# A Nyström attention and sticky expert kernel: two batches put on one Newton chain, and all order tables written anew

## The chip, the cores and the metric

The kernel runs on one core of a Trainium2 chip. The metric is device time in microseconds (us) of one execution; the time before is the median of three. Engines are called as in the profile: PE (TensorE matmul), PEld (its weight loads), DVE (VectorE), ACT (ScalarE), POOL (GpSimd), SP (SyncE, which here only issues loads).

## The reference

There are 8 batches (B), 8 heads, 576 tokens (S) and a head width of 64. First comes Nyström attention with 32 landmarks, the means of 18 tokens each:

```python
q_lm = q.reshape(B, H, m, S // m, D).mean(axis=3)
k_lm = k.reshape(B, H, m, S // m, D).mean(axis=3)
A = sm(q, k_lm)          # sm: softmax of the scaled product
Bm = sm(q_lm, k_lm)      # 32 x 32 for each head
C = sm(q_lm, k)
Z = Bm.transpose(0, 1, 3, 2) / (norm1(Bm) * norminf(Bm) + 1e-06)
for _ in range(6):
    Z = 2 * Z - Z @ Bm @ Z
return A @ Z @ C @ v
```

The loop is a Newton iteration for the pseudo-inverse of `Bm`: six steps, each of which needs the one before it, on one 32x32 matrix for each head and batch. The attention's result, 576 rows of 512 numbers for each batch, then goes to a mixture of 8 experts. A token takes the expert with its own largest gate value, or, where a local gate is at least 0.5, the expert of the token before it; its output is `p[e] * (relu(x @ w1[e]) @ w2[e])`, with `w1` 512x1024 and `w2` 1024x512.

## The kernel before

Each batch has a piece of attention and an expert run. The expert run takes the expert that most tokens of the batch chose ("votes") and runs all 576 tokens through it; tokens that chose another one are gathered into an additional short run (the "slot"), which stands between batches 6 and 7. Products of the expert run are made in three terms, since both factors are split in a high and a low part: `ath`, `atl` of the attention, `gh`, `gl` of the first weights, `h` (its two halves) and `wh`, `wl` of the second weights. L737 multiplies the attention with the first weights into the "ph" banks; ACT (L746) makes the relu and DVE (L749, L752) its low half; L790 and L781 multiply `h` with the second weights into "py" and "pg". A product of L737 can only be written to a ph bank whose relu and low half are done. The first weights of a batch are not `w1` itself but `w1` multiplied by the attention's folded value matrix `wt`; that product is L694, eight long products (sixteen passes of 32 rows) for one half of the weights.

The expert run of a batch is cut in 16 chunks. The attention of later batches is put into it piece by piece: `PLANS[b]` holds, for each step of batch b in the order of `STEPS`, the chunk at which the step is emitted, counted from the start of the run of batch b-1 (`SECOND` and `FIRST` do it for batches 1 and 0, `SLOT_AT` for the slot, `G_AT` for L694, `W2_AT` for some loads). From this emitted order a list scheduler with a cost model sets the order of each engine's queue, which is then fixed. `in_row` ties matmuls together so that nothing is put between them; `one` gives, in turn, the three small PSUM banks in which all small products land.

The steps that the change touches: `norms` (scales `Bm`, transposes it to `bt`, and makes the factor `nrc`), `nf` (`newton_first`, L420 product and L424 sums) and `n0` to `n5` (`newton_step`, L432 product and L435 sum). A Newton step is one "trip" here: eight small products on PE (sixteen passes in the trace, 32x32 weights and 64 columns, 32 in the last step), then one DVE sum of 128x2x64. Before, a batch's state `et` moves on through four tiles `et0` to `et3` that all batches share in turn (`next_et`). Other names below: L482 are the scores of `A` (8 products for half a batch) and L487 turns them over, L304 the scores of `C` with L317 and L319 their exponentials, L331 transposes of `C`, L345 its product with `v`, L493 to L505 the softmax of `A`, L516 and L520 the split of its result in `ath` and `atl` (128x1152), L590 to L593 the votes, L241 and L242 the landmark sums, L671 the loads of the first weights.

Of the kernel before, what the change touches and what calls it, by code (L numbers as in the profile page):

```python
# [9 lines left out]
F32 = mybir.dt.float32  # L10
# [4 lines left out]
ALU = mybir.AluOpType  # L15
# [22 lines left out]
JOINT = 3  # L38

# [37 lines left out]
def nystrom_attn_then_sticky_moe(ctx, tc, qT, kT, v, wg, w12, out):  # L77
# [291 lines left out]
    ets = [const.tile([P, 2, 96], F32, name=f"et{i}") for i in range(4)]  # L369
# [3 lines left out]
    def next_et():  # L373

        ets.append(ets.pop(0))
        return ets[-1]

    def norms(b, st):
# [5 lines left out]
        et = st["et"] = next_et()  # L384
# [17 lines left out]
        nrc = st["nrc"] = sm.tile([P, 2], F32, name="nrc")  # L402
# [896 lines left out]
    SECOND = dict(v=3.6, q0=0.1, k0=0.6, c0=0.6, q2=0.1, k2=1.1, c1=1.6, norms=2.6, a0=6.1, nf=7.1, a1=7.1, t0=7.6,
        amax=7.6, n0=7.6, t2=7.6, n1=7.6, t4=7.6, aexp=8.6, n2=7.6, cv=7.6, n3=7.6, n4=8.1, anorm=8.6, n5=8.1, nw=8.1,  # L1300
        gw=8.1, aback=8.6, gates=8.6, nwt=12.6, votes=8.6, split=10.1, w1=8.6, w1b=9.7, fresh=10.1, sticky=11.1,
        chosen=14.6, own=21.1)
# [3 lines left out]
        2: (-13.9, -11.4, -10.4, -13.4, -7.9, -9.4, -7.9, -7.4, -7.4, -6.4, -7.4, -4.4, -2.4, -4.9, -1.4, -1.4, 1.6,  # L1306
            -0.4, -1.4, -0.4, 0.1, 0.1, 1.6, -2.4, 6.6, 5.1, 5.1, 6.1, 6.6, 6.6, 8.1, 13.6, 8.1, 8.1, 9.1, 13.6,
            14.6),
        3: (-23.4, -16.9, -20.9, -13.4, None, -14.4, -14.4, -13.4, -13.4, -9.9, -8.4, -8.9, -6.4, -7.9, -3.4, -7.9,
            -8.4, -6.4, -7.9, -3.4, -2.9, -3.9, -2.4, -2.4, 1.1, 1.6, 1.6, 1.6, 3.6, 4.1, 3.6, 4.6, 8.6, 4.6, 6.1,  # L1310
            12.1, 12.6),
# [132 lines left out]
```

## Time and profile before

| what | us |
|---|---|
| median of 3 runs | 471.43 (471.01, 471.43, 475.08) |
| the profiled execution | 472.64 |
| its span | 470.9 |
| PE busy in the span | 456.2 (97%) |
| DVE, ACT, POOL busy | 272.0, 203.4, 233.1 |
| granted clock, mean | 0.996 of 2.4 GHz |

The span is what the profile covers; the execution's own time is 1.7 us longer. Matmuls are pipelined: one starts before the last has ended, so the distance from start to start is what a matmul takes from PE's time, not its own duration. Such distances are read from the timeline of PE, where each line gives the start, the busy time of the group, and in brackets how long the engine was idle before it.

### The profile page before, as it was taken

To read this page: it belongs to the slowest core of one execution; us is meant where nothing else is said; L and a number is where in the kernel's file an instruction comes from. 1 tells how busy PE (TensorE), PEld (TensorE's weight loads), DVE (VectorE), ACT (ScalarE), POOL (GpSimd) and SP (SyncE) were. 2 spreads that over 40 slices of the span, in tenths; PEclk is the share of its full clock that TensorE was granted. 3 is DMA by queue.
4 is the path that set the end of the run, shared out by engine and by line. 5 is a ranking of instruction groups with operands and counts; after the bars stand their busy time and mean duration, and the time that the engine had idled before them with its cause. 6 is when DMAs were issued, how large, how long until landed. Compare 5 with 4: busy or idle time off the path is not lost.

```text
span 470.9 us, 12133 instructions
## 1 busy us (share of the span) xinstructions
PE 456.2 (97%) x4709; PEld 338.3 (72%) x4709; DVE 272.0 (58%) x825; ACT 203.4 (43%) x516; POOL 233.1 (50%) x364
## 2 busy tenths in 40 slices
PE   8989999999999999999999999999999999999995
PEld 3546667687776777767886677767885887778884
DVE  6897866876586548548633575338548933523231
ACT  2456245554344616355245634354333613555121
POOL 7187582395374508448613544055426864467000
PEclk9999999999999999999999999999999999999998
DMA  8993383991497227937842244333532911762011
GB/s 305 316 376 127 114 308 104 359 336 59 148 321 254 90 73 253 366 89 249 316 135 74 92 173 178 126 96 110 205 107 58 321 43 48 235 218 75 1 57 47
DMA packets 38717, 82.01 MB, mean 174 GB/s; under 512 B 3275, under 2 KB 4555, under 8 KB 37888
## 3 DMA queue, kind: packets, MB, share of 16 engines
q1 hardware_dynamic: 31920, 66.70, 41.4%
q10 hardware_dynamic: 5248, 9.44, 5.7%
q0 software_dynamic: 1488, 5.07, 2.8%
q8 instruction: 38, 0.62, 0.5%
q14 instruction: 23, 0.19, 0.1%
HBM read 66.29 MB, written 14.94 MB: 173 GB/s over the span
## 4 chain that ended last, share of the span: by engine, by line
PE 81%; DVE 7%; DMA 3%; ACT 3%; issue 2%; POOL 2%; SPq 0%; POOLq 0%; ACTq 0%; DVEq 0%
PE py L790 36%; PE ph L737 21%; PE pg L781 5%; PE ph L694 3%; PE one L432 2%; PE one L345 2%; DMA k_t<-kT 2%; PE one L482 2%; PE one L331 2%; DMA q_t<-qT 1%; PE one L304 1%; POOL t L241 1%; ACT ec L317 1%; PE one L570 1%; DVE h L749 1%
## 5 line engine op out<-in xcount | busy, mean ns | idle before, releaser
L790 PE MATMUL py<-wh,h 128*128 128x512 f32 x528 | 171.9, 402 | 0.2
L725 POOL TENSOR_TENSOR wl<-raw,wh 128x512 fp32r<-128x512 f32 x68 | 87.0, 1298 | 70.1 <-ACT wh L720 62.2
L790 PEld LDWEIGHTS py<-wh,h 128*128 128x128 f32 x528 | 95.5, 188 | 28.7 <-issue 7.0
L746 ACT ACTIVATE h<-ph 128x256 fp32r<-128x256 f32 (+2 forms) x136 | 54.6, 402 | 133.1 <-PE ph L737 111.2
L749 DVE SCALAR_TENSOR_TENSOR h<-ph,h 128x256 fp32r<-128x256 f32 (+1 forms) x136 | 55.6, 410 | 81.4 <-ACT h L746 80.2
L790 PE MATMUL py<-wl,h 128*128 128x512 f32 x264 | 90.7, 393 | 0.0
L737 PE MATMUL ph<-ath,gh 128*128 128x320 f32 (+1 forms) x256 | 79.9, 312 | 2.5 <-DVE h L749 1.5
L737 PE MATMUL ph<-atl,gh 128*128 128x320 f32 (+1 forms) x256 | 75.9, 297 | 0.4 <-DVE atl L530 0.4
L737 PE MATMUL ph<-ath,gl 128*128 128x320 f32 (+1 forms) x256 | 76.0, 297 | 0.0
L737 PEld LDWEIGHTS ph<-ath,gh 128*128 128x128 f32 x256 | 48.1, 188 | 19.9 <-issue 6.2
L790 PEld LDWEIGHTS py<-wl,h 128*128 128x128 f32 x264 | 49.5, 188 | 10.3 <-issue 0.8
L737 PEld LDWEIGHTS ph<-atl,gh 128*128 128x128 f32 x256 | 48.2, 188 | 4.2 <-DVE atl L530 0.7
L737 PEld LDWEIGHTS ph<-ath,gl 128*128 128x128 f32 x256 | 48.1, 188 | 0.5 <-issue 0.3
L720 ACT CAST wh<-raw 128x512 fp32r<-128x512 f32 x68 | 41.1, 630 | 9.2 <-DMA raw<-w 8.8
L811 ACT ACTIVATE ys<-py,pall 128x512 f32<-128x512 f32 x30 | 20.0, 689 | 11.5 <-DMA out<-ys 7.5
L494 POOL TENSOR_TENSOR sa<-sa,mxa 128x1152 f32<-128x1152 f32 x7 | 14.9, 2133 | 19.8 <-DVE mxa L493 19.7
L707 ACT CAST gh<-ph 128x512 fp32r<-128x512 f32 (+1 forms) x19 | 10.6, 564 | 28.0 <-PE pg L694 26.2
L241 POOL TENSOR_TENSOR t<-k_t 128x288 f32<-128x288 f32 x24 | 19.6, 838 | 5.7 <-DMA k_t<-kT 1.6
L781 PE MATMUL pg<-wl,h 128*128 128x512 f32 x56 | 22.4, 400 | 0.0
L241 POOL TENSOR_TENSOR t<-q_t 128x288 f32<-128x288 f32 x28 | 20.4, 748 | 3.7 <-DVE sk L242 1.3
L781 PE MATMUL pg<-wh,h 128*128 128x512 f32 x56 | 22.2, 397 | 0.0
L435 DVE TENSOR_TENSOR et<-one,et 128x128 f32<-128x128 f32 (+1 forms) x42 | 11.3, 270 | 15.1 <-PE one L432 14.9
(337 smaller groups left out, 726.2 us busy)
## 6 DMA issues: line engine op xcount, KB each, us to landing
raw<-w SPq DMA_DIRECT2D x68, 256.0 KB, 5.1
raw<-w SPq DMA_DIRECT2D x17, 1024.0 KB, 7.1
v_t<-v SPq DMA_DIRECT2D x8, 1024.0 KB, 6.7
out<-ys ACTq DMA_DIRECT2D x32, 256.0 KB, 2.9
q_t<-qT SPq DMA_DIRECT2D x6, 1152.0 KB, 5.5
k_t<-kT SPq DMA_DIRECT2D x6, 1152.0 KB, 8.4
ad<-sa POOLq DMA_DIRECT2D x8, 576.0 KB, 3.3
q_t<-qT SPq DMA_DIRECT2D x4, 576.0 KB, 8.0
```

Of the source, the lines that this page charges most:

```text
L241: nc.gpsimd.tensor_add(t9[:, i], src[:, a + i, :, 0:9], src[:, a + i, :, 9:18])
L435: nc.vector.tensor_tensor(out=half(new, 1), in0=half(pn, 1), in1=half(et, 2), op=ALU.add)
L494: nc.gpsimd.tensor_tensor(out=sa, in0=sa, in1=mx.unsqueeze(2).broadcast_to([P, 2 * NJ, M]), op=ALU.subtract)
L694: mm = nc.tensor.matmul(ps[g][32 * c:32 * c + 32, 0:n * P], w, w1[r, n * i:n * i + n, a * P:a * P + P], start=True, stop=True)
L720: cut = nc.scalar.copy(out=wh, in_=raw)
L725: nc.gpsimd.tensor_tensor(out=wl, in0=raw, in1=wh.bitcast(F32), op=ALU.subtract)
L737: mm = nc.tensor.matmul(hp, w[:, g, c], x[:, g, s0:s0 + n], start=(i == 0), stop=(i == 5))
L746: nc.scalar.activation(out=h[:, 0:e], in_=hp[:, 0:e], func=AF.Relu)
L749: nc.vector.scalar_tensor_tensor(out=h[:, 384:384 + m], in0=hp[:, 0:m], scalar=0.0, in1=h[:, 0:m].bitcast(F32), op0=ALU.max, op1=ALU.subtract)
L781: nc.tensor.matmul(yps[4], hs[ff][1], w, start=(ff == 0 and w is w2[ff][0]), stop=(ff == NC2 - 1 and w is w2[ff][1]))
L790: mms.append(nc.tensor.matmul(yps[full[i]], h[:, part + i * P:part + i * P + P], w, start=(f == 0 and part == 0 and w is wh), stop=(f == N ...
L811: nc.scalar.mul(out=ys, in_=yp, mul=st["pw"][:, k:k + 1])
```

## The change

Batches 4 and 5 share one Newton chain (`PAIR = {4:5}`). Their states lie side by side in one tile of four matrices' width (`[P, 4, 96]`, of which there are now three instead of four tiles of half the width), and their factors in one tile `nrc4`. The first product and the six steps are emitted once, with batch 4's steps: a trip has 16 products tied in a row and one sum of 128x4x64. Batch 5's seven entries in its plan become None. Any other batch swaps its state twice for each step and thereby updates it in place. All tables are written anew.

```diff
+PAIR = {4:5}
-    ets = [const.tile([P, 2, 96], F32, name=f"et{i}") for i in range(4)]
+    ets = [const.tile([P, 4, 96], F32, name=f"et{i}") for i in range(3)]
...
-    def next_et():
-
-        ets.append(ets.pop(0))
-        return ets[-1]
+    def next_et(b):
+        bs = sorted((b, partner.get(b, b)))
+        if b not in used:
...
+        else:
+            for x in bs:
+                used[x] = used[x][::-1]
+        for x in bs:
+            kept[x % 2] = used[x][0]
+            sts[x]["et"] = ets[used[x][0]][:, 2 * (x % 2):2 * (x % 2) + 2]
+        return ets[used[b][0]][:, 0:4] if b in PAIR else sts[b]["et"]
...
     def newton_step(b, st, k, meanwhile=None):
         n = 64 if k < 5 else 32
-        et = st["et"]
-        pn = chain(b).tile([P, 2, 64])
-        each_place(lambda g, r: nc.tensor.matmul(pn[r, g, 0:n], et[r, g, 32:64], et[r, g, 0:n], start=True, stop=True))
-        new = st["et"] = next_et()
+        w = 4 if b in PAIR else 2
+        et = ets[used[b][0]] if b in PAIR else st["et"]
+        pn = chain(b).tile([P, w, 64])
+        mms = []
+        for q in range(0, w, 2):
+            each_place(lambda g, r: mms.append(nc.tensor.matmul(
+                pn[r, q + g, 0:n], et[r, q + g, 32:64], et[r, q + g, 0:n], start=True, stop=True)))
+        if b in PAIR:
+            in_row(mms)
+        new = next_et(b)
...
-        4: (-25.4, -20.9, -19.4, -18.4, None, -16.9, -16.9, -15.9, -15.4, -15.4, -14.9, -14.4, -11.9, -12.4, -10.4,
-            -6.9, -8.4, -7.9, -5.9, -8.4, -6.4, -5.9, -4.9, -6.9, -4.9, -5.4, -5.4, -3.9, 2.6, 4.1, 2.6, 2.6, 4.6,
+        4: (-25.4, -21.9, -19.9, -18.4, None, -17.4, -18.9, -15.9, -15.4, -15.4, -4.9, -14.4, -11.9, -4.4, -10.4,
+            -6.9, -1.4, -7.9, -6.9, -1.9, -6.9, -0.4, -4.4, -0.4, -4.4, 1.1, 1.6, 2.1, 2.6, 4.6, 2.6, 1.6, 4.6, 3.1,
```

So batch 4's Newton steps move from chunks -14.9 to -5.4 to chunks -4.9 to 1.1. The order of PE is the same up to about 87 us of the trace of before, differs from there to about 246 us, and is again the same to the end but for two short stretches (near 285 and 416 us). PE runs the same set of products; DVE has six instructions fewer and POOL one. Three places show what moved; lines of the new file are numbered some 50 higher (L694 becomes L746, L432 L481, L435 L487, L520 L572, L737 L789, L749 L801, L790 L842, L331 L334, L345 L348).

PE, before, at batch 2's first weights (`raw`, L694; near 141 us of the trace):

```order
L694 MATMUL pg<-raw_2084,wt 32x512
L694 MATMUL ph<-raw_2084,wt 32x512
L432 MATMUL one<-et_176 32x64 x8
L345 MATMUL one<-v_t,ect 32x64 x40
L624 LDWEIGHTS er
L624 MATMUL one<-identb,er 128x5
L625 LDWEIGHTS er
L625 MATMUL one<-identb,er 128x5
L432 MATMUL one<-et_177 32x64 x8
L694 MATMUL pg<-raw_2084,wt 32x512
```

The same place after:

```order
L842 MATMUL py<-wh,h 128x512 x2
L842 MATMUL py<-wl,h 128x512 x2
L746 MATMUL ph<-raw_2072,wt 32x512
L746 MATMUL pg<-raw_2072,wt 32x512
L746 MATMUL ph<-raw_2072,wt 32x512
L746 MATMUL pg<-raw_2072,wt 32x512
L746 MATMUL ph<-raw_2072,wt 32x512
L746 MATMUL pg<-raw_2072,wt 32x512
L746 MATMUL ph<-raw_2072,wt 32x512
L746 MATMUL pg<-raw_2072,wt 32x512
L789 MATMUL ph<-ath,gh 128x256
```

Before, two Newton trips and the product with `v` stand between the fifth and the sixth of the eight products; after, the eight stand together.

DVE, before, at the split of batch 2's attention (`atl`, near 129 to 133 us; `et` is the Newton state of batch 3):

```order
L435 TENSOR_TENSOR et_178<-one,et_176 128x2x64
L592 MAX top<-tot 128x8
L593 MAX_INDEX regs<-top,tot 128x8
L502 TENSOR_REDUCE rsa<-sa 128x36
L749 SCALAR_TENSOR_TENSOR h<-ph,h 128x256 x2
L242 TENSOR_REDUCE sq<-t_2812 128x64
L503 TENSOR_SCALAR rsa<-rsa 128x36
L435 TENSOR_TENSOR et_179<-one,et_178 128x2x64
L618 TENSOR_SCALAR old<-one 5x128
L520 TENSOR_TENSOR atl<-at,ath 128x1152
```

The same place after:

```order
L644 MAX top<-tot 128x8
L645 MAX_INDEX regs<-top,tot 128x8
L801 SCALAR_TENSOR_TENSOR h<-ph,h 128x256 x2
L487 TENSOR_TENSOR et_177<-one,et_177 128x2x64
L572 TENSOR_TENSOR atl<-at,ath 128x1152
L554 TENSOR_REDUCE rsa<-sa 128x36
L245 TENSOR_REDUCE sq<-t_2644 128x64
L555 TENSOR_SCALAR rsa<-rsa 128x36
L487 TENSOR_TENSOR et_177<-one,et_177 128x2x64
```

Before, two Newton sums of batch 3 stand ahead of `atl`; after, the second one stands behind it and behind two reductions.

PE, before, at the end of batch 4's Newton steps (near 189 to 193 us; the L694 are batch 3's first weights):

```order
L790 MATMUL py<-wl,h 128x512
L432 MATMUL one<-et_179 32x64 x8
L345 MATMUL one<-v_t,ect 32x64 x40
L432 MATMUL one<-et_176 32x64 x8
L694 MATMUL ph<-raw_2913,wt 32x512
L694 MATMUL pg<-raw_2913,wt 32x512
```

After, at the next half of the same first weights:

```order
L789 MATMUL ph<-atl,gh 128x256
L789 MATMUL ph<-ath,gl 128x256
L842 MATMUL py<-wh,h 128x512 x2
L481 MATMUL one<-et_176 32x64 x16
L746 MATMUL ph<-raw_2872,wt 32x512
L746 MATMUL pg<-raw_2872,wt 32x512
```

Trips of 8 products that belonged to batch 4 alone have become trips of 16 for both batches, later in the program.

## Rows read from the trace of the kernel before

**Rows 1.** Windows: length; busy PE, PEld, DVE, ACT, POOL; clock; DMA share; GB/s.

```profile
87.00:246.00 159.00, 157.53 (x1817) 118.74 (x1818) 101.39 (x299) 74.73 (x186) 89.39 (x125) 1.00 0.61 211
```

**Rows 2.** Timeline of PE at batch 2's and batch 3's first weights.

```profile
141.07 0.61 PE L694 MATMUL ph<-raw,wt 64*32 64x512 f32 x1
...
142.07 0.43 PE L432 MATMUL one<-et 32*32 32x64 f32 x16
...
144.57 0.61 PE L694 MATMUL pg<-raw,wt 64*32 64x512 f32 x1
...
145.56 0.38 PE L737 MATMUL ph<-ath,gh 128*128 128x256 f32 x1
...
192.77 0.61 PE L694 MATMUL ph<-raw,wt 64*32 64x512 f32 x1
...
193.79 0.50 PE L790 MATMUL py<-wh,h 128*128 128x512 f32 x1
```

**Rows 3.** Timeline of PE at the scores of batch 5 and of an earlier batch.

```profile
50.50 0.71 PE L482 MATMUL one<-q_t,k_t 64*32 64x288 f32 x16
51.14 0.73 PE L790 MATMUL py<-wh,h 128*128 128x512 f32 x2
...
210.75 1.16 PE L482 MATMUL one<-q_t,k_t 64*32 64x288 f32 x18
212.10 0.71 PE L482 MATMUL one<-q_t,k_t 64*32 64x288 f32 x14 [0.19 <-DVE sa L487]
212.74 0.74 PE L570 MATMUL one<-at,wgc 128*32 128x160 f32 x16
```

**Rows 4.** Timeline of PE around one Newton trip of batch 5.

```profile
242.85 0.42 PE L432 MATMUL one<-et 32*32 32x64 f32 x16
243.21 0.50 PE L790 MATMUL py<-wh,h 128*128 128x512 f32 x1
```

**Rows 5.** The source line L432, all passes: duration ns min/median/max.

```profile
L432 PE MATMUL one<-et x672: 191/214/239, 59.2 to 354.5; 32*32 32x64 f32 x140, 32*32 32x32 f32 x28
```

**Rows 6.** Timeline of PE at a Newton trip of batch 3 in two pieces.

```profile
135.95 0.41 PE L432 MATMUL one<-et 32*32 32x64 f32 x12
136.30 0.50 PE L790 MATMUL py<-wh,h 128*128 128x512 f32 x1
...
137.88 0.30 PE L432 MATMUL one<-et 32*32 32x64 f32 x4
138.11 0.50 PE L790 MATMUL py<-wh,h 128*128 128x512 f32 x1
```

**Rows 7.** Timeline of PE at its longest wait between 87 and 246 us.

```profile
187.21 0.40 PE L790 MATMUL py<-wl,h 128*128 128x512 f32 x1
188.80 0.38 PE L737 MATMUL ph<-ath,gh 128*128 128x256 f32 x1 [1.19 <-DVE h L749]
```

**Rows 8.** Timeline of DVE and POOL at that wait.

```profile
185.47 2.94 DVE L520 TENSOR_TENSOR atl<-at,ath 128x1152 fp32r<-128x1152 f32 x1
...
186.48 2.53 POOL L241 TENSOR_TENSOR t<-k_t 128x288 f32<-128x288 f32 x2
```

**Rows 9.** The source line L520: duration ns min/median/max.

```profile
L520 DVE TENSOR_TENSOR atl<-at,ath x7: 1316/1349/2940, 80.8 to 375.0; 128x1152 fp32r<-128x1152 f32 x7
```

**Rows 10.** Timeline of DVE and ACT behind the scores of batch 3.

```profile
110.01 0.21 DVE L311 TENSOR_REDUCE mx<-ph 128x1 f32<-128x64 f32 x1
...
111.01 0.28 ACT L319 ACTIVATE bm<-ph,nm 128x32 f32<-128x32 f32 x1
```

**Rows 11.** The loads of first weights (L671) on SP, and their landing.

```profile
182.85 0.97 SPq L671 DMA_DIRECT2D raw<-w  x2
222.19 0.98 SPq L671 DMA_DIRECT2D raw<-w  x2
...
DMA to landing us min/median/max: 4.1/5.7/11.6
```

**Rows 12.** Timeline of PE at batch 4's first weights.

```profile
249.87 0.61 PE L694 MATMUL ph<-raw,wt 64*32 64x512 f32 x1
```

More of the change, by code (lines that the diff above doesn't have):

```diff
@@ L367, in c_sums, with nrc_of @@
                                 in1=parity.unsqueeze(2).broadcast_to([P, 2, 2]), op=ALU.mult)
-    ets = [const.tile([P, 2, 96], F32, name=f"et{i}") for i in range(4)]
+    ets = [const.tile([P, 4, 96], F32, name=f"et{i}") for i in range(3)]
     for et in ets:
         nc.gpsimd.memset(et[:, :, 64:96], 0.0)
-    def next_et():
-        ets.append(ets.pop(0))
-        return ets[-1]
+    partner = {**PAIR, **{y: x for x, y in PAIR.items()}}
+    kept, used = {}, {}
+    def next_et(b):
+        bs = sorted((b, partner.get(b, b)))
+        if b not in used:
+            taken = [kept.get(x % 2) for x in bs]
+            free = [i for i in range(3) if i not in taken]
+            for x in bs:
+                used[x] = free[0], [i for i in range(3) if i != free[0]]
+            others = sorted(used[b][1], key=lambda i: i in taken and (1 + taken.index(i)))
+            for x in bs:
+                used[x] = free[0], others[0]
+        else:
+            for x in bs:
+                used[x] = used[x][::-1]
+        for x in bs:
+            kept[x % 2] = used[x][0]
+            sts[x]["et"] = ets[used[x][0]][:, 2 * (x % 2):2 * (x % 2) + 2]
+        return ets[used[b][0]][:, 0:4] if b in PAIR else sts[b]["et"]
+    nrcs = {}
+    def nrc_of(b):
+        k = min(b, partner[b])
+        if k not in nrcs:
+            nrcs[k] = sm.tile([P, 4], F32, name="nrc4")
+        return nrcs[k][:, 2 * (b % 2):2 * (b % 2) + 2]
     def norms(b, st):
@@ L383, in norms @@
         bm = st["bm"]
-        et = st["et"] = next_et()
+        if b not in used:
+            next_et(b)
+        et = st["et"]
         bt = st["bt"] = sm.tile([P, 2, M], F32, name="bt")
@@ L416, in newton_first @@
     def newton_first(b, st):
+        if b in PAIR:
+            ps = one.tile([P, 4, M])
+            two = sts[b], sts[PAIR[b]]
+            mms = []
+            for q, t in enumerate(two):
+                each_place(lambda g, r: mms.append(nc.tensor.matmul(
+                    ps[r, 2 * q + g, :], t["bt"][r, g, :], t["bt"][r, g, :], start=True, stop=True)))
+            in_row(mms)
+            yield
+            for q, t in enumerate(two):
+                for g in range(2):
+                    nc.vector.scalar_tensor_tensor(out=t["et"][:, g, 32:64], in0=ps[:, 2 * q + g], scalar=t["nrc"][:, g:g + 1],
+                                                   in1=id32, op0=ALU.mult, op1=ALU.add)
+            return
         ps = chain(b).tile([P, 2, M])
@@ L1297, in at_time @@
         events.append((t, len(events), fn))
[L1299 to L1302, printed above, removed]
+    SECOND = dict(v=2.6, q0=0.1, k0=0.1, c0=0.6, q2=0.6, k2=0.1, c1=1.6, norms=3.6, a0=6.1, nf=7.1, a1=7.1, t0=7.6,
+        amax=7.6, n0=7.6, t2=7.6, n1=7.6, t4=7.6, aexp=7.6, n2=7.6, cv=7.6, n3=7.6, n4=8.1, anorm=8.6, n5=8.1, nw=8.1,
+        gw=8.1, aback=8.6, gates=8.6, nwt=12.6, votes=8.6, split=11.1, w1=8.6, w1b=10.7, fresh=12.1, sticky=13.1,
+        chosen=15.6, own=20.6)
     STEPS = ("load v q0 k0 c0 q2 k2 c1 norms a0 nf a1 t0 n0 t2 amax n1 t4 aexp n2 cv n3 anorm n4 aback n5 "
@@ L1305, in nystrom_attn_then_sticky_moe @@
     PLANS = {
[L1306 to L1311, printed above, removed]
@@ L1327, in nystrom_attn_then_sticky_moe @@
+    SLOT_AT = (-17.5, -3.5, -7.0, -6.5, -2.0, 3.0, 1.5, 8.5, 6.6, -0.5, 25.0)
     TURN = 6
[L1328 to L1330 removed]
+    FIRST = dict(rs=0.1, rm=0.6, re=0.6, rn=2.1, rb=2.6, gw=1.1, gates=3.6, votes=4.1, fresh=6.6, sticky=6.6,
+        chosen=6.6, own=8.1)
+    W2_AT = (10, 11, 14, 14, 15, 15)
     IN_ROW = 9
```

36 lines of the change are left out of this document (21 added, 15 removed).

## The prediction, made before the changed kernel ran

> **What bounds the kernel now.** I read first the windows, then the timeline of PE inside the window that the change touches. The order of PE changes only between 87 and 246 us, so that window says what there is to win: of its 159.00 us PE is busy 157.53, at a granted clock of 1.00, while DVE is busy 101.39, ACT 74.73, POOL 89.39 [rows 1]. The reader is to see two things. PE is idle there for only 1.5 us, so a wait taken away can bring 1.5 us and no more; and 1.19 us of it is a single wait, of a product of the expert run on DVE [rows 7]. Whatever else the change brings must come from PE's own work: the set of products is the same before and after, so not from fewer products, but from how they stand in the queue. For that the timeline of PE has to be read by distances from start to start. Groups of small products (32 or 64 rows) start close together and fill different parts of the array at once; each time such a group is cut or put somewhere else, it pays its ramp again. DVE, with 0.64 of the window, has room on average, but it matters where a long instruction of it stands in front of a short one that PE waits for.
>
> One reference for all that follows: the durations are those of the profiled execution of 472.64 us. It was 1.21 us above the median of 471.43, so I make the sum against 472.64 and take 1.21 off at the end.
>
> **First weights of batch 2 made whole.** Before, the eight products of L694 near 141 us are cut in five and three by two Newton trips and the product with v. The five take 1.00 us (142.07 - 141.07), the three 0.99 (145.56 - 144.57); all eight of batch 3, uncut, take 1.02 (193.79 - 192.77) [rows 2]. A few products more or less cost nothing as long as they overlap. The order of after has the eight in one piece: 1.00 + 0.99 - 1.02 = **-0.97 us**, all of it PE time and so on the path. I see no bound above or below but the reading of a start, 0.1 us.
>
> **Scores of batch 5 taken apart.** Before, both halves (L482) stand back to back: 212.74 - 210.75 = 1.99 us, with a wait of 0.19 for the turning by DVE (L487) of the first half, whose bank the second reuses. A half by itself, between products of the expert run, takes 51.14 - 50.50 = 0.64 [rows 3]. After, the halves stand apart: 2 x 0.64 - 1.99 = **-0.71 us**. The cover is the expert products that now stand between them; it would be -0.5 if one of the halves came behind other small work.
>
> **Six shared trips.** A trip of sixteen passes takes 243.21 - 242.85 = 0.36 us of PE [rows 4]. Its group is busy 0.42 us while a single pass is busy 0.214 [rows 4, 5], so the sixteen starts are spread over 0.21 us, and the remaining 0.15 is ramp, paid once for each trip. A shared trip of 32 passes then takes 0.15 + 2 x 0.21 = 0.57 against 2 x 0.36 = 0.72: -0.15, six times **-0.9 us**. The first product is not merged: the order has its two parts as two groups of eight. The bounds are 0 (each half pays all its own) and -0.9. I take -0.9, since the spread is a row and the ramp is what remains of it. A rule speaks against this part. The Trainium skill, TensorEngine Tiling (Array Packing), Instruction Overhead, says that each matmul costs some 60 cycles on trn2 however few its columns; as an estimate from that page, 16 passes more would cost 16 x 60 / 2.4 GHz = 0.40 us, a shared trip 0.76, and the sharing would save nothing. The trace does not agree: sixteen starts in 0.21 us are 13 ns each, half of it.
>
> The chain itself is not on the path: in the order of after 2.7 to 3.7 us of PE work stand between one shared trip and the next, and what has to fit in is one sum on DVE. So the serial length of one chain against two costs and saves nothing. DVE loses six short sums and gets six wider ones, which PE does not wait for.
>
> **Cut trips.** Three trips of batches 3 and 5 stood in two pieces before. One such: 0.35 + 0.23 = 0.58 us (136.30 - 135.95, 138.11 - 137.88) against 0.36 for a whole one [rows 6, 4], so 0.22 for a cut. After, none of these is cut, but the scores of C (L304), whose last eight products were cut once before, are cut twice. Net two cuts fewer: **-0.44 us**, bounds -0.2 and -0.7. The number of places where small work interrupts the expert run is otherwise about the same (104 before, 105 after by the order), so nothing is left over there.
>
> **The wait at 188.80.** A product of L737 waits 1.19 us for the low half of a relu (L749) [rows 7]. It comes from DVE: the split `atl` of batch 3 took 2.94 us there, and the relu's half stood behind it in DVE's queue [rows 8]; the same instruction took 1.349 us in the median of seven [rows 9]. Beside it POOL worked on 2.53 us of landmark sums [rows 8]. In the order of after `atl` of batch 3 stands at another point, with 3.6 us and more of PE work between the relu and its products. So **-1.19 us**, with 0 as the bound on the other side.
>
> **New: the Newton sum behind `atl`.** After, batch 3's second Newton sum stands behind `atl`, a reduction over 1152 and a landmark reduction on DVE, where before it stood ahead of `atl`. Its trip's bank is taken next by transposes of C (L331) that follow with about 0.7 us of PE work between. So PE waits until DVE comes to the sum. With `atl` at its median, 1.349, I work out 0.2 to 0.7 us; with 2.94 [rows 9] 1.8. I take **+0.7 us**, as the median lies near the shortest of the seven (1.316), and keep 0.2 and 1.8. What is queued behind this sum on DVE is the scan of the sticky choice and later halves of the relu, which have over 3 us of PE work ahead of them. As to which of the two lengths comes: the 2.94 stood beside POOL's sums, as rows 8 show. The Trainium skill, SBUF - State Buffer, Who interferes with whom, states that a DVE instruction with two SBUF inputs contends with a GpSimd one that reads SBUF, and that the loser is blocked for the whole of the other's instruction; rows 8 and 9 agree with it (2.94 against 1.349), and where POOL's sums fall beside the moved `atl` the term would by that rule be the upper one and the sum 1.1 us worse.
>
> **New: a ph bank reused early.** Batch 5's scores of C put part of their result in a ph bank that the expert run wants again after 1.5 us of PE work. For batch 3 the chain from DVE's first reduction to the end of ACT's `bm` took 111.01 + 0.28 - 110.01 = 1.28 us [rows 10], and before that DVE must be free. That gives 0 if DVE is free at once, 0.8 if it is as late as at batch 3, where 1.0 us passed first. I take the middle, **+0.4 us**.
>
> **What costs nothing.** Batch 5's loads are issued four chunks earlier, into free q and k buffers; no product waits for a load in this window. In-place update of the other batches' states, `nrc4` and the memset that is gone move no wait. The short stretches after 246 us change no term.
>
> **Sum.** -0.97 - 0.71 - 0.9 - 0.44 - 1.19 + 0.7 + 0.4 = -3.1 us: 469.5 against 472.64, **468.3 us** against the median, 0.7% less. That is inside the 1% that a measurement of this kernel can tell from no change. Best ends of all terms: -0.97 - 0.71 - 0.9 - 0.7 - 1.19 + 0.2 = -4.3; worst: -0.9 - 0.5 - 0.2 + 1.8 + 0.8 = +1.0, about 472.4.
>
> **Rivals.** (A) The new waits do not show, because DVE is free earlier than the order lets one see, and the remaining 0.3 us of idle PE goes too. For it: 36% of DVE is free [rows 1], and the small groups that keep their place may overlap better. Against: two places with under 1.5 us of cover. -3.1 - 1.1 - 0.3 = -4.5, 466.9; only beyond that lies a gain over 1%. (B) Slower than before: batch 4's first weights come late. Before, its loads of w1 were issued at 222.19 and used at 249.87, 27.7 us later [rows 11, 12]. The votes now come right behind the shared chain, and by the order only about 10.9 us of PE work stands between the vote and that product. Batch 3 had 192.77 - 182.85 = 9.9 us from issue to use [rows 2, 11] and did not wait, which speaks against; the longest landing of these loads was 11.6 [rows 11], which speaks for. If they land so late, PE waits 1.7 us; if in addition each of the six steps of the chain is held up by half an `atl` (6 x 0.7 = 4.2), 5.9 in all. From 3.1 us on it is slower than before; at 5.9 it gives 468.3 + 5.9 = 474.2. (C) Sharing saves nothing, because 32 passes take twice as long as 16: the change then acts through its tables alone, +0.9, 469.2. By the page named above it would be this one; the 13 ns between starts speak against it. That the change does not do what it says is excluded by the order, which has six groups of 32 passes.
>
> **Chances.** The forecast 0.5, A 0.25, C 0.15, B 0.1. Of A somewhat over half goes beyond 1%, since gains that I cannot name lie there too, and of the forecast's own spread a little: faster by over 1% (below 466.7) 0.2. B goes over 1% (above 476.1) only if both lateness terms are exceeded, with unnamed losses 0.05. The range leaves out the far ends of A and B: 465.4 to 472.6.
>
> **What would show it.** In the profile of after: a whole L746 group of 1.0 us at batch 2; score halves of 0.64 us each; shared trips with 0.57 us from start to start (0.72 would be C); no wait over 1 us where 188.80 was; new waits of PE for a Newton sum (L487) near 133 us and for ACT or DVE behind the scores (L307) near 180; no wait at batch 4's first weights (one of over 3 us would be B). I am wrong if the stretch before 87 us or behind 246 us changes by over 1 us, since nothing moved there, or if other `atl` now stretch to 2.9 us.

## The result, and the profile of the changed kernel

The changed kernel takes 474.78 us (median of 9 runs, 473.53 to 476.24), the kernel before, beside it, 471.98 (471.01 to 475.08): a ratio of 1.0055, 95% interval 1.0031 to 1.0079. It is 0.55% or 2.6 us slower, where 0.7% faster was forecast. The profiled execution has a span of 473.0 against 470.9, at a clock of 0.999 against 0.996, so the clock is not it.

What the prediction costed did happen. The timeline of PE after shows the first weights of batch 2 whole (142.78 to 143.80, 1.02 us from start to start, where [rows 2] had 1.00 + 0.99), a shared trip of 32 passes (201.17 to 201.75, 0.58, where two of [rows 4] make 0.72), and a half of batch 5's scores by itself (208.69 to 209.34, 0.65, where [rows 3] had 1.99 for two).

```profile
142.78 0.61 PE L746 MATMUL ph<-raw,wt 64*32 64x512 f32 x1
...
143.80 0.39 PE L789 MATMUL ph<-ath,gh 128*128 128x256 f32 x1
...
201.17 0.65 PE L481 MATMUL one<-et 32*32 32x64 f32 x32
201.75 0.61 PE L746 MATMUL ph<-raw,wt 64*32 64x512 f32 x1
...
208.69 0.71 PE L534 MATMUL one<-q_t,k_t 64*32 64x288 f32 x16
209.34 0.50 PE L842 MATMUL py<-wh,h 128*128 128x512 f32 x1
```

The window of [rows 1] after, in the same columns:

```profile
87.00:246.00 159.00, 156.12 (x1762) 118.10 (x1762) 102.42 (x292) 75.43 (x187) 88.96 (x125) 1.00 0.57 196
```

PE is idle for 2.88 us of it, where it was idle for 1.47: one wait of 1.19 went [rows 7], and more came. PE's waits after, from 87 us to 460 (total, times, longest); the kernel before has three groups here, all on DVE (1.2, 0.7 and 0.2 us), and none on ACT:

```profile
PE py L842 <- ACT ys L863: 1.5, 2, 0.9
PE py L842 <- ACT h L798: 1.3, 2, 0.7
PE ph L746 <- DVE h L801: 0.7, 1, 0.7
PE one L334 <- DVE et L487: 0.4, 1, 0.4
PE one L481 <- DVE et L470: 0.3, 1, 0.3
PE one L481 <- DVE et L487: 0.3, 1, 0.3
PE ph L746 <- DMA raw<-w: 0.2, 1, 0.2
```

The first two lines, 2.8 us, are products with the second weights that wait for ACT: for the relu (`h`), their factor, or for the scaling of an output block (`ys`), which empties the bank that they write. In PE's timeline they are these four, and two behind sums of batch 3's Newton chain:

```profile
114.75 0.73 PE L842 MATMUL py<-wh,h 128*128 128x512 f32 x2 [0.73 <-ACT h L798]
...
132.68 0.47 PE L481 MATMUL one<-et 32*32 32x64 f32 x16 [0.35 <-DVE et L470]
...
137.81 0.41 PE L334 MATMUL one<-ident,ec 128*64 128x128 f32 x2 [0.36 <-DVE et L487]
...
194.95 0.50 PE L842 MATMUL py<-wh,h 128*128 128x512 f32 x1 [0.91 <-ACT ys L863]
...
396.91 0.50 PE L842 MATMUL py<-wh,h 128*128 128x512 f32 x1 [0.54 <-ACT ys L863]
...
417.06 0.50 PE L842 MATMUL py<-wh,h 128*128 128x512 f32 x1 [0.55 <-ACT h L798]
```

Where the time goes is read by comparing the starts of the same product of the expert run in both traces. At 86 us, where the orders part, PE is 0.1 us ahead of the kernel before; at 253 us it is 0.5 ahead, at 395.6 level; behind the wait at 396.91 it is 0.62 late, behind 421 us 1.5, at the last product 1.73 (466.45 against 464.72). So there are two misses: the window of the change brings 0.4 us where the sum had 3.1, and the rest of the program, which the prediction put at nothing, loses 2.3 us, most of it at the two waits of the end.

### The profile page after: what moved, and what is told of

Its sections match the earlier page's. It is cut to its first block, busy times and chain, and to the rows that moved or that the text cites. A ratio compares the mean times of both kernels' runs of the same rounds, so it can differ in the third digit from the quotient of the medians.

```text
span 473.0 us, 12119 instructions
## 1 busy us (share of the span) xinstructions
PE 454.2 (96%) x4705; PEld 336.7 (71%) x4709; DVE 273.3 (58%) x819; ACT 203.5 (43%) x516; POOL 233.7 (49%) x363
## 4 chain that ended last, share of the span: by engine, by line
PE 71%; DVE 10%; DMA 8%; ACT 5%; issue 2%; POOL 2%; SPq 0%; ACTq 0%; DVEq 0%; POOLq 0%
PE py L842 33%; PE ph L789 19%; PE pg L833 5%; DMA k_t<-kT 4%; PE ph L746 2%; PE one L481 2%; DMA out<-ys 2%; PE one L534 2%; PE one L348 1%; PE one L334 1%; DMA q_t<-qT 1%; PE one L307 1%; POOL wl L777 1%; DMA raw<-w 1%; DVE h L801 1%
## 5 line engine op out<-in xcount | busy, mean ns | idle before, releaser
L842 PE MATMUL py<-wh,h 128*128 128x512 f32 x528 | 172.8, 402 | 2.8 <-ACT ys L863 1.5
L777 POOL TENSOR_TENSOR wl<-raw,wh 128x512 fp32r<-128x512 f32 x68 | 88.0, 1311 | 70.3 <-ACT wh L772 66.8
L842 PEld LDWEIGHTS py<-wh,h 128*128 128x128 f32 x528 | 95.8, 188 | 32.9 <-issue 8.4
L801 DVE SCALAR_TENSOR_TENSOR h<-ph,h 128x256 fp32r<-128x256 f32 (+1 forms) x136 | 55.6, 410 | 82.6 <-ACT h L798 76.9
L842 PE MATMUL py<-wl,h 128*128 128x512 f32 x264 | 90.8, 393 | 0.0
L789 PE MATMUL ph<-ath,gh 128*128 128x320 f32 (+1 forms) x256 | 80.2, 313 | 1.2 <-DVE hx L804 0.8
L789 PE MATMUL ph<-atl,gh 128*128 128x320 f32 (+1 forms) x256 | 76.3, 298 | 0.5 <-DVE atl L582 0.5
L789 PE MATMUL ph<-ath,gl 128*128 128x320 f32 (+1 forms) x256 | 76.0, 297 | 0.0
L789 PEld LDWEIGHTS ph<-ath,gh 128*128 128x128 f32 x256 | 48.1, 188 | 19.3 <-issue 5.2
L842 PEld LDWEIGHTS py<-wl,h 128*128 128x128 f32 x264 | 49.4, 188 | 10.5 <-issue 0.9
L789 PEld LDWEIGHTS ph<-atl,gh 128*128 128x128 f32 x256 | 48.1, 188 | 4.2 <-DVE atl L582 0.7
L789 PEld LDWEIGHTS ph<-ath,gl 128*128 128x128 f32 x256 | 48.3, 189 | 0.7 <-issue 0.5
L863 ACT ACTIVATE ys<-py,pall 128x512 f32<-128x512 f32 x30 | 20.2, 687 | 14.9 <-DMA out<-ys 8.5
L546 POOL TENSOR_TENSOR sa<-sa,mxa 128x1152 f32<-128x1152 f32 x7 | 14.9, 2134 | 18.8 <-DVE mxa L545 18.8
L244 POOL TENSOR_TENSOR t<-q_t 128x288 f32<-128x288 f32 x28 | 21.5, 790 | 3.1 <-DVE sq L245 1.3
L760 DVE TENSOR_TENSOR gl<-ph,gh 128x512 fp32r<-128x512 f32 (+1 forms) x19 | 12.4, 658 | 17.8 <-ACT gh L759 17.8
L244 POOL TENSOR_TENSOR t<-k_t 128x288 f32<-128x288 f32 x24 | 17.4, 744 | 9.5 <-DMA k_t<-kT 5.5
```

Of the source, the lines that this page charges most:

```text
L244: nc.gpsimd.tensor_add(t9[:, i], src[:, a + i, :, 0:9], src[:, a + i, :, 9:18])
L546: nc.gpsimd.tensor_tensor(out=sa, in0=sa, in1=mx.unsqueeze(2).broadcast_to([P, 2 * NJ, M]), op=ALU.subtract)
L760: last = nc.vector.tensor_tensor(out=gl[:, g, x], in0=ps[g][:, 0:n * P], in1=gh[:, g, x].bitcast(F32), op=ALU.subtract)
L777: nc.gpsimd.tensor_tensor(out=wl, in0=raw, in1=wh.bitcast(F32), op=ALU.subtract)
L789: mm = nc.tensor.matmul(hp, w[:, g, c], x[:, g, s0:s0 + n], start=(i == 0), stop=(i == 5))
L801: nc.vector.scalar_tensor_tensor(out=h[:, 384:384 + m], in0=hp[:, 0:m], scalar=0.0, in1=h[:, 0:m].bitcast(F32), op0=ALU.max, op1=ALU.subtract)
```

## Experiments

Theories as the expectations number them (the changed kernel is called "after", as in the profile lines): **1**, the loss sits in new waits of PE for ACT, made by the rewritten tables (1a `G_AT`, 1b the slot's steps); **2**, the shared chain itself costs; **3**, the new state tiles and the in-place update cost; **4**, what the shared chain gains is given back where ACT's output scaling waits for a store; **5**, it is given back elsewhere.

**State code alone, and the pair alone.** The first has all old tables and no pair; the second adds the pair and the new entries of batches 4 and 5 alone.

```diff
-PAIR = {4:5}
+PAIR = {}
...
-    SLOT_AT = (-17.5, -3.5, -7.0, -6.5, -2.0, 3.0, 1.5, 8.5, 6.6, -0.5, 25.0)
+    SLOT_AT = (-15.5, -3.0, -7.0, -4.0, -2.5, 3.5, 1.5, 9.0, 6.6, -1.5, 26.0)
...
```

All other tables go back to those of before in the same way. The second differs from this one by `PAIR = {4:5}` and by the entries 4 and 5 of `PLANS`, which are those of after.

> The new code for the states (three wide tiles, states updated in place) with the pair switched off and all tables of before. Theory 1 (the loss sits in new waits of PE on ACT, made by the rewritten tables): as before, 472.0 within 0.7 us. Theory 2 (the shared chain itself costs): also 472.0, since nothing is shared here. Theory 3 (the new tiles and the in-place update cost): near 474.8.

> Pair on, the new tables for batches 4 and 5 only, all other tables of before, so the order is that of before up to about 160 us and from about 253 us on. Theory 1: the six shared trips give 0.9 us and the score halves 0.7, the wait at 188.80 of before may go (1.2) and the wait for the output at 194.95 of after may come (0.9), the waits near 115, 397 and 417 us of after are not there: 470.5, between 469.5 and 471.5. Theory 2: 474 or more, since the sharing is all there. Theory 3: 474 or more.

The first: 471.96, ratio 1.0007 (0.9990 to 1.0023). Theory 3 is out. The second: 471.78, 0.9998 (0.9987 to 1.0010), outside theory 1's range and far from the 474 of the two others. So the shared chain by itself is neither gain nor loss; but in the traces PE gains 1.1 us on the first between 85 and 253 us, and has lost these and 0.5 more at the last product. The pair brings something, and something takes it back.

**All new tables, no sharing.** The entries of batch 5's chain that were None are filled, so that it runs by itself.

```diff
-PAIR = {4:5}
+PAIR = {}
...
-        5: (-30.9, -22.4, -30.4, -27.9, None, -22.9, -22.4, -21.9, -21.4, -16.9, None, -16.4, -10.4, None, -10.4,
+        5: (-30.9, -22.4, -30.4, -27.9, None, -22.9, -22.4, -21.9, -21.4, -16.9, -20.9, -16.4, -10.4, -20.4, -10.4,
...
```

> The changed kernel with the pair switched off: batches 4 and 5 make their own trips of 16 passes, one behind the other at the places where the shared trips stood; all other tables are the new ones. Theory 1: six trips more at 0.15 us, so 0.9 us slower than the changed kernel, 475.7. Theory 2: faster than the changed kernel by the 2.8 us that it lost, near 472. The other rival of the prediction, that sharing saves nothing on PE: 474.8, no change.

474.18, 1.0048 (1.0031 to 1.0066). Slow without any sharing: theory 2 is out. The 0.9 us that the shared trips save did not come back as a loss either, so theory 1's 475.7 missed; the 0.6 us between this run and after lies within the intervals. In the traces the run without sharing loses 0.7 us on after between 196 and 290 us, where the chain stands, but the order of other products differs there too, so this is no measure of the sharing alone. PE waits at the same places as after (0.94 us for `ys` at 192.95, 0.54 at 395.71, 0.51 for `h` at 415.78).

**The tables of the end.** First both are put back as they were before, then `G_AT` alone, then `SLOT_AT` alone; all else is as after.

```diff
-    G_AT = {0: (14, 15), 1: (14, 15), 2: (13, 15), 3: (14, 15), 4: (10, 13), 5: (13, 15), 6: (13, 14), 7: (3, 7)}
+    G_AT = {0: (14, 15), 1: (14, 15), 2: (13, 15), 3: (14, 15), 4: (10, 13), 5: (13, 15), 6: (13, 14), 7: (2, 7)}
-    SLOT_AT = (-17.5, -3.5, -7.0, -6.5, -2.0, 3.0, 1.5, 8.5, 6.6, -0.5, 25.0)
+    SLOT_AT = (-15.5, -3.0, -7.0, -4.0, -2.5, 3.5, 1.5, 9.0, 6.6, -1.5, 26.0)
```

> The changed kernel with the old tables for the slot and its first weights alone (the first half of batch 7's first weights one chunk earlier, the slot's steps as before), so only the order from about 395 us on changes. Theory 1: the wait of PE on ACT near 417 us goes (0.9 us with what lies around it), the one near 397 us (0.6) perhaps as well: 473.3 to 473.9. Theories 2 and 3: 474.8, no change.

> The changed kernel with the first half of batch 7's first weights put back one chunk earlier, nothing else. Putting back all slot tables gave 2.5 us. Theory 1a (the first weights were the cover for ACT's relu, which stands behind a cast that waits for a load; moved behind the relu's product they cover nothing): takes most of it, 472.3 to 473.3, and the wait of PE near 417 us is gone from the trace. Theory 1b (the slot's own steps, half to two and a half chunks earlier or later, cost it): 474.2 or more.

> The changed kernel with the old table of the slot's steps and the new place of batch 7's first weights. Theory 1a: 473.9 to 474.8, the wait near 397 us (0.6) gone at most. Theory 1b: 472.3 to 473.3.

Both: 472.29, 1.0008 (0.9992 to 1.0024). `G_AT` alone: 473.54, 1.0032 (1.0011 to 1.0052). `SLOT_AT` alone: 472.98, 1.0029 (1.0008 to 1.0050). From 1.0055 that is 2.2, 1.1 and 1.2 us. For both together the interval lies apart from that of after, and the effect is larger than expected; for each alone the intervals overlap, and the time with `G_AT` old fell between the ranges of 1a and 1b. The split is read from the traces, by the starts of the same products: after loses 1.7 us on the run with both tables old, 0.8 at 396.91 and 0.9 between 415 and 421 us; it loses 0.9 at the second place alone on the run with `G_AT` old, and 0.8 at the first alone on that with `SLOT_AT` old. So each table costs its part, and the parts add up. With `G_AT` old the wait at 417 is gone and that at 397 stays; with `SLOT_AT` old it is the other way round. This is theory 1, with both its parts.

How `G_AT` does it is seen on ACT. Its timeline after, where the relu that PE waits for at 417.06 is queued behind a cast that waits for its load, and behind an output scaling:

```profile
415.64 0.62 ACT L772 CAST wh<-raw 128x512 fp32r<-128x512 f32 x1 [0.72 <-DMA raw<-w]
415.73 0.34 ACTq L864 DMA_DIRECT2D out<-ys  x1
416.16 0.68 ACT L863 ACTIVATE ys<-py,pall 128x512 f32<-128x512 f32 x1
416.75 0.27 ACT L798 ACTIVATE h<-ph 128x128 fp32r<-128x128 f32 x1
```

Before, that cast stood behind the scaling and the relu:

```profile
414.71 0.28 ACT L746 ACTIVATE h<-ph 128x128 fp32r<-128x128 f32 x1
...
415.23 0.62 ACT L720 CAST wh<-raw 128x512 fp32r<-128x512 f32 x1 [0.24 <-ACT h L746]
```

And half of batch 7's first weights stood on PE just there, 1.0 us of work that needs nothing of the relu (timeline of PE before):

```profile
414.21 0.28 PE L737 MATMUL ph<-xah,gl 128*128 128x128 f32 x1
414.42 0.61 PE L694 MATMUL ph<-raw,wt 64*32 64x512 f32 x1
...
415.44 0.50 PE L790 MATMUL py<-wh,h 128*128 128x512 f32 x1
```

The new table puts that half behind the waiting product, at 417.73: the cover is gone. It also moves the cast: in the three runs with the new `G_AT` (after, without sharing, `SLOT_AT` old) the cast stands ahead of the scaling and the relu, in those with the old one behind them. Which of the two is worth how much was not separated. With `SLOT_AT`, POOL's last gather for the slot starts at 392.12 where it started at 390.99; ACT's next relu starts at 394.49 (before 393.87) though the products that it reads start 0.2 us earlier than before, and the scaling queued behind it ends as PE's product at 396.91 starts.

```profile
394.49 0.38 ACT L798 ACTIVATE h<-ph 128x256 fp32r<-128x256 f32 x1 [4.38 <-PE pg L833]
394.90 0.69 ACT L868 ACTIVATE ys<-pg,pall 64x512 f32<-64x512 f32 x1
395.60 0.68 ACT L873 ACTIVATE yl<-pg,pall 64x512 f32<-64x512 f32 x1
396.19 0.67 ACT L863 ACTIVATE ys<-py,pall 128x512 f32<-128x512 f32 x1
```

Why the relu follows the gather is not shown: in three runs it starts 2.33 to 2.37 us behind the start of the last gather (392.12 to 394.49 after, 390.93 to 393.29 without sharing, 392.62 to 394.95 with `G_AT` put back), and no row names the gather as its releaser. The relu waits for a signal of PE, and in these three traces PE's signal comes while the rows of the last gather land (394.42 after, landing from 394.18 to 394.49), 0.8 us behind the end of the products; in the kernel before the gather had landed by 393.38 and the signal came at 393.80, right behind the products. Why a signal of PE should come with a landing stays open.

**Where the pair's gain goes: all stores short.** The pair alone has a wait of 1.23 us for `ys`, and `ys` waits for a store.

```profile
193.16 0.50 PE L842 MATMUL py<-wh,h 128*128 128x512 f32 x1 [1.23 <-ACT ys L863]
```

Both kernels with the stores of batches 1 to 5 cut to 16 rows:

```diff
-            nc.scalar.dma_start(out=out[t0:t0 + P, :], in_=ys)
+            n = P if b in (0, 6, 7) else 16
+            nc.scalar.dma_start(out=out[t0:t0 + n, :], in_=ys[0:n])
```

> Pair on with the tables of the second run (batches 4 and 5 new, the rest of before), and the output of batches 1 to 5 stored only in the first 16 rows of each block, so seven eighths of it are left out and these stores are short. Theory 4 (the 1.2 us that PE gains by 252 us is given back behind it, where ACT's output scaling waits for an earlier store to land and ACT's queue holds up PE): at least 0.8 us faster than the same cut without the pair. Rival theory 5 (it is given back for another reason, at the slot's loads or in the pace of the products): no more than 0.3 faster than the same cut without the pair.

> The kernel before with the same cut of the stores (seven eighths of the output rows of batches 1 to 5 are left out): the partner of the run above. Theory 4: within 0.4 us of before, since PE waits for no store there. Theory 5: the same; the difference between the two runs decides.

With the pair 470.24, 0.9966 (0.9954 to 0.9979); without 472.54, 1.0014 (1.0001 to 1.0026). The pair is worth 2.3 us there. But with so many sizes changed the order of the queues moved as well, so narrower cuts followed.

**A third output buffer.** It takes the wait away without leaving work out; room for it comes from the zeros of the warm-up products, one column read over and over. In the pair alone, the kernel before, and after with the old tables of the end:

```diff
-    zeros = const.tile([P, 512], BF16, name="zeros")
+    zeros = const.tile([P, 2], BF16, name="zeros")
...
-        ys = fk.tile([P, DM], F32, name="ys", bufs=2)
+        ys = fk.tile([P, DM], F32, name="ys", bufs=3)
```

> Pair on with the tables of the second run, the whole output stored, and a third buffer for the scaled output rows (to make room, the zeros that warm PE at the start are one column read over and over). The scheduler then orders ACT and what hangs on it anew from 145 us on. Theory 4 (what PE gains is given back where ACT waits for a store to land): ACT waits for stores no more, PE has no wait of 0.9 to 1.2 us for output scaling near 192 us, and it is 0.8 us or more faster than the same buffers without the pair; near 470.5 in all. Theory 5 (given back elsewhere): within 0.5 us of the same buffers without the pair.

> The kernel before with the same third buffer and the same zeros: the partner of the run above. Theories 4 and 5: within 0.7 us of before, 471.3 to 472.7, since no wait of PE for a store is in its trace; more only by what the new order does elsewhere.

> The changed kernel with the old slot tables and the third buffer. Theory 4: the wait near 194 us (0.9) goes and so does the hold-up of ACT near 295 us (0.3 on PE): about 1.2 us faster than with two buffers, 471.1. Theory 5: 472.3, no change.

479.44, 1.0177 (1.0146 to 1.0207); 479.13, 1.0166 (1.0142 to 1.0190); 477.07, 1.0092 (1.0067 to 1.0117). The expectations missed widely: ACT's output scaling does not wait for stores any more, but everything is ordered anew, and the three are 5 to 7 us slower. With and without the pair they differ by 0.3 us, far within the noise of six and five runs. They tell nothing of theory 4.

**Two short stores, and a load moved.** The last store (64 rows) of batches 2 and 4 cut to 16 rows, in the pair alone and in the kernel before; and, in the pair alone, the load of batch 5's `v` put behind loads of second weights, in the trace 20 us later (204.57 for 184.29), in case it held up the store.

```diff
-            nc.scalar.dma_start(out=out[t0:t0 + 64, :], in_=ys[0:64])
+            n = 16 if b in (2, 4) else 64
+            nc.scalar.dma_start(out=out[t0:t0 + n, :], in_=ys[0:n])
```

```diff
-        5: (-30.9, -22.4, -30.4, -27.9, None, -22.9, -22.4, -21.9, -21.4, -16.9, None, -16.4, -10.4, None, -10.4,
+        5: (-30.9, -15.9, -30.4, -27.9, None, -22.9, -22.4, -21.9, -21.4, -16.9, None, -16.4, -10.4, None, -10.4,
...
+        if b == 5:
+            not_ahead_of(i, "w2")
```

> Pair on with the tables of the second run; the stores of the last, short block of batches 2 and 4 write 16 of their 64 rows, the other 48 are left out. No engine's order changes. Theory 4: the wait of PE near 192 us (1.2 us) is gone and ACT waits less near 293 us: at least 0.8 us faster than the same cut without the pair, 470.9 or less. Theory 5: within 0.4 us of it.

> The kernel before with the same two stores cut: the partner. Both theories: as before within 0.3 us, since PE waits for no store there.

> Pair on with the tables of the second run, nothing left out; SP issues batch 5's load of v some 14 us later, behind the first loads of the next second weights, where the store near 187 us has landed. Only SP's order changes. Theory 4, with the load of v as the cause of the late store: the wait near 192 us shrinks by half or more, 470.6 to 471.3, faster than before. Theory 4 without that cause (the loads of first and second weights alone hold the store up): the wait stays at 1.0 us or more and the time at 471.8. Theory 5: 471.8.

472.11, 0.9998 (0.9981 to 1.0015); 471.86, 0.9994 (0.9979 to 1.0008); 472.05, 1.0001 (0.9981 to 1.0022). I had cut the wrong store: ACT's `ys` still waits 1.97 us, until 193.86, and PE 1.87 for it. And the load is not the cause: with it moved `ys` still waits 1.29 us, until 192.34, and PE 1.2.

**The right store short.** The store that `ys` waits for is that of batch 2's third block. 112 of its 128 rows, and 48 of the 64 of the last block, stored beside it, are left out, in the pair alone and in the kernel before.

```diff
-            nc.scalar.dma_start(out=out[t0:t0 + P, :], in_=ys)
+            n = 16 if b in (2,) and k in (2,) else P
+            nc.scalar.dma_start(out=out[t0:t0 + n, :], in_=ys[0:n])
...
+            n = 16 if b in (2,) else 64
```

> Pair on with the tables of the second run; for batch 2 alone, the store of the third block and that of the last, short block write 16 rows and leave out the others (112 of 128, 48 of 64). No engine's order changes. Theory 4: the wait of PE near 192 us (1.2 us) is gone in the trace, and in the median the run is 0.6 us or more faster than its partner without the pair; the rest may be lost at the slot's load near 412 us (0.5). Theory 5: within 0.3 us of the partner.

> The kernel before with the same two stores cut: the partner. Both theories: as before within 0.3 us.

With the pair 470.65, 0.9972 (0.9959 to 0.9985); without 471.92, 1.0001 (0.9986 to 1.0016). The same cut, with no instruction moved, gives the pair 1.2 us and the kernel before nothing. Theory 4 is shown for this wait. ACT in the pair alone:

```profile
183.97 0.34 ACTq L864 DMA_DIRECT2D out<-ys  x1
...
192.42 0.69 ACT L863 ACTIVATE ys<-py,pall 128x512 f32<-128x512 f32 x1 [1.33 <-DMA out<-ys]
```

and with the short store:

```profile
192.03 0.72 ACT L863 ACTIVATE ys<-py,pall 128x512 f32<-128x512 f32 x1
```

The store issued at 183.97 landed 8.4 us later, and on this `ys` starts. In the kernel before, the one issued at 184.48 landed 6.9 us later, at 191.4, when ACT's `ys` started,

```profile
184.48 0.34 ACTq L812 DMA_DIRECT2D out<-ys  x1
...
191.39 0.68 ACT L811 ACTIVATE ys<-py,pall 128x512 f32<-128x512 f32 x1
```

and no product waited: PE was that late itself, by its 1.19 us at 188.80 [rows 7]. So the wait that the pair takes away comes back 4 us later, as a wait for the store. PE's waits with the short store, from 87 to 460 us, name ACT no more:

```profile
PE ph L746 <- DVE h L801: 0.7, 1, 0.7
PE ph L789 <- DVE gl L760: 0.2, 1, 0.2
PE one L481 <- DVE et L487: 0.2, 1, 0.2
```

This wait is not all that takes the gain back. The 1.1 us that the pair alone is ahead at 253 us are counted behind it; with the short store the lead on the partner there is 2.4 us. Behind 253 us the pair alone loses 1.6 us by its trace: 0.4 near 295, where ACT's scaling waits 3.06 us for another store ahead of the casts of first weights, 0.6 at 413.67, where ACT has waited for a load, and the rest little by little, most of it by a slower pace ("Open" below). With the short store it still loses 0.7 near 295. No run isolates these losses.

**A buffer for that scaling alone.** In the pair alone, with whole output, one `ys` of its own for the scaling at 192.42; beside it the small zeros by themselves, which its room asks for.

```diff
-    zeros = const.tile([P, 512], BF16, name="zeros")
+    zeros = const.tile([P, 2], BF16, name="zeros")
...
-        ys = fk.tile([P, DM], F32, name="ys", bufs=2)
+        ys = fk.tile([P, DM], F32, name="ys3", bufs=1) if (b, k) == (2, 3) else fk.tile([P, DM], F32, name="ys", bufs=2)
```

> Pair on with the tables of the second run, the whole output stored; the scaled rows of batch 2's fourth block have a buffer of their own, so this one scaling need not wait for the store issued near 184 us (room for it comes from the zeros that warm PE at the start, one column read over and over). PE's order changes at the start and between about 190 and 207 us only. Theory 4: the wait near 192 us is gone and it is 0.6 to 1.3 us faster than the run with the small zeros alone, 470.7 if those cost nothing. Theory 5: no difference between the two.

> The partner of the run above: pair on with the tables of the second run, the small zeros and nothing else. 471.8 if the zeros cost nothing.

With both 474.68, 1.0061 (1.0042 to 1.0080), with the zeros alone 475.61, 1.0074 (1.0053 to 1.0095). The 0.9 us between the medians is within theory 4's range, but the intervals overlap, and in the traces the whole difference arises before 101 us, long before the buffer is used. The run with the zeros alone has no wait for `ys` near that place either, so these two tell nothing of theory 4. The small zeros cost 3.6 us against the pair alone by the ratios. The three longest waits of PE between 25 and 62 us with them:

```profile
PE ph L789 <- DVE eq L636: 1.8, 1, 1.8
PE one L622 <- DVE at L1164: 1.5, 1, 1.5
PE one L676 <- DVE er L672: 0.8, 1, 0.8
```

None of them stands in the pair alone: a smaller tile, with the same products, and the order of DVE, ACT and POOL at the gates of the first batches is another. PE falls 4.5 us behind the pair alone between 25 and 63 us, part of it at a lower clock (last section). With the buffer beside them the waits are 1.8, 1.0 and 0.7, and PE falls 2.4 us behind. The kernel before with the third output buffer has the same three (1.8, 1.5, 0.7) and loses 2.2 us there, of 6.1 in all by its trace; so about a third of that loss is this and not the buffer. No kernel with the whole output that beats both came out of the runs.

## Why the prediction was wrong

**The step that failed** is the one in "What costs nothing": "The short stretches after 246 us change no term." They cost 2.3 us by the traces. I took them for nothing because few rows of PE's order differ there, and asked of each move how PE's and DVE's queues stand. I never asked what the first weights, one entry in the table, stood in front of, nor how ACT's queue is ordered there: a relu behind a cast that waits for a load. Putting the two tables of the end back gained 2.2 us, 1.7 by the traces. My own sign of being wrong, that the stretch "behind 246 us changes by over 1 us", came. The other sentence of that paragraph, that the states' new code moves no wait, held: its run is level with the kernel before.

**The second miss** is of the same kind: in the sum ACT appears only for the scores of C. Its output scaling has two buffers, and a product whose bank it is to empty waits for a store to land. It cost 1.2 us in the pair alone, as the short store shows; after has 0.91 at the same place. The scores of batch 3 at 114.75 are a third such wait, 0.73: ACT does their exponentials from 111.23 to 113.81 in a row, then `ql` and the scaling of `et`, and starts the relu at 114.24; before, the relu came at 113.15, ahead of two such steps. No run isolates this one.

**What held.** First weights whole: -0.97 forecast, 1.02 for 1.99 measured. Halves of the scores apart: 0.65 and 0.64 each, as forecast. The wait at 188.80 went. The new wait behind `atl`: +0.7 forecast, 0.36 measured at 137.81, inside its bounds, as `atl` took its short length there, 1.42. Another 0.35 at 132.68, on the first sums, was not foreseen and fills the term: DVE had those sums behind a `psum` scaling of 128x5 that took 2.86 us there (median of eight 0.17), and that ended with a POOL instruction on `sa` (130.31 to 132.44). Two other `atl` took 2.60 and 2.42 us, and no product waited for them. The one for the ph bank (+0.4) did not show.

**The shared trip**: 0.57 forecast, 0.58 measured, with 0.58 as well at 208.11 and 216.18; rival C would have had 0.72. The Trainium skill, TensorEngine Tiling (Array Packing), Instruction Overhead, would make it, as an estimate from its 60 cycles for each matmul added to the 0.36 of one trip, 0.76; the trace does not agree, 32 passes that fill different parts of the array take 0.58 with their ramp.

**The sum in the window** was off by 2.7 us (0.4 for 3.1). Waits of PE grew by 1.41 where -0.28 was forecast (+0.7 + 0.4 - 1.19, and the 0.19 within the scores' term); 1.64 of what came are the two waits for ACT, and 0.26 at 100.08 (a sum) and 0.24 at 89.33 (a load) were not foreseen either. The gain of 0.4 then leaves 1.41 + 0.41 = 1.82 us of PE's own work saved, of 2.83 forecast. Added up by kind from start to start, without the waits, the named pieces are there: Newton trips 1.25 less (0.9 + 0.44 forecast), first weights 0.94, scores 0.76. But the expert run's first products (L789), the same 294, take 0.90 us more, and the transposes (L334) 0.38. So the term that failed is "nothing is left over there"; why those products take longer is open.

**Rivals.** B, late first weights of batch 4, did not come: they start at 249.47 with no wait. B, at 0.1, was the only rival on the slower side; it was reached by another way, waits on ACT, that no rival had.

**Open**: from 280 to 400 us, products of the second weights that follow each other stand 230.5 and 231.0 ns apart in the pair alone (means of two stretches of 60 us), and 228.9 and 229.3 in the kernel before; up to the end some 300 such products make this 0.5 us. It goes with the sharing: all thirteen kernels with the pair have 229.9 to 231.0 there, the seven without it 228.7 to 229.6, the one with all new tables and no sharing too (229.3 and 229.4). Its cause is not found. The pair alone further waits 0.54 us at 413.67 behind a cast that waits for a load (2.49 us), a place where PE being early buys nothing, as the load lands when it lands.

## What to carry to other kernels

Before moving filler work on the bounding engine, ask what it covers: walk back from the product behind it through the queues of the other engines, to loads and to stores that have to land before a buffer is free. A gain on the bounding engine counts only up to the next place that is tied to a transfer; look at the landing times of stores, not only of loads, and at how many output buffers there are. And when one change brings a feature and new tables for everything, time the feature with the old tables first: here it was free, and the tables cost 2.7 us, 2.2 of them the two of the end.

## What of the hardware was unexpected

The landing of a store: 2.8 us in the median of the 30 stores of L864 in the pair alone, 8.4 for the one that decided. The DMA view of that kernel from 184 to 192.5 us (busy tenths; what was issued, KB, median us to landing):

```profile
DMA  9999999999946156689999989999999999999999
...
v_t<-v SPq DMA_DIRECT2D x1, 1024.0 KB, 11.2
out<-ys ACTq DMA_DIRECT2D x1, 256.0 KB, 8.4
```

The engines are full but for some 2 us, and ACT stands still for the store that came in between. Moving that load of 1024 KB did not bring it in earlier, so what of the transfers held it up stays open.

And a clock that fell in one run and not in another with the same waits. With the small zeros PE was busy 7.66 of the 10 us from 40 on, and in the next 10 the granted clock was 0.83 of 2.4 GHz in the mean, so part of it ran at 1.2:

```profile
40.00:50.00 10.00, 7.66 (x54) 5.30 (x46) 8.29 (x17) 4.76 (x17) 9.53 (x13) 1.00 0.21 69
50.00:60.00 10.00, 8.21 (x72) 5.64 (x75) 6.75 (x30) 1.58 (x7) 3.07 (x11) 0.83 0.31 109
```

With the buffer beside the small zeros PE was busy 7.52 of the same 10 us, even less, and the clock stayed at 1.00, as it did in the pair alone (9.09 busy). So the waits alone do not tell whether the clock falls, and what made it fall here is not shown:

```profile
40.00:50.00 10.00, 7.52 (x54) 5.30 (x46) 8.97 (x21) 4.75 (x17) 9.04 (x13) 1.00 0.26 82
50.00:60.00 10.00, 8.95 (x86) 6.39 (x87) 8.31 (x34) 1.63 (x7) 3.36 (x12) 1.00 0.34 109
```
